# Linear attention and a gated feed-forward layer on one core: queries in two layouts, softmax statistics through DRAM

## The chip, the cores and the metric

The kernel runs on one core of a Trainium2 chip. The time is the device time of one execution in microseconds (us). The core has five instruction streams that run beside each other: TensorE (PE in the profile; its weight loads are PEld), VectorE (DVE), ScalarE (ACT), GpSimd (POOL) and SyncE (SP), which here issues all DMAs. Sixteen DMA engines move the data. Matrix products go to PSUM; everything else that is computed lies in SBUF.

## The reference

```python
def attn(q, k, v):                       # each (8, 8, 576, 64), float32
    q_s = exp(q - max(q, axis=-1));  q_s /= sum(q_s, axis=-1) + 1e-9     # over the 64 channels
    k_s = exp(k - max(k, axis=2));   k_s /= sum(k_s, axis=2) + 1e-9      # over the 576 tokens
    kv = einsum('bhsd,bhse->bhde', k_s, v)
    return einsum('bhsd,bhde->bhse', q_s, kv)

x = attn(q, k, v).transpose(0, 2, 1, 3).reshape(4608, 512)
out = ((x @ w_a) * (x @ w_b)) @ w_out    # w_a, w_b (512, 1536), w_out (1536, 512), float64
```

A query's softmax runs over channels, a key's over tokens. So where tokens lie on partitions, a query's maximum is one along the row and a key's one across partitions; where channels lie on partitions it is the other way round.

## The kernel before

The 4608 tokens are taken in nine chunks c of T = 512. Two heads at a time make a group g of 128 channels, four groups in all. A chunk has two halves of work. *Attention* gives xf[c], the chunk's input to the feed-forward layer with channels on partitions, one tile px of 128x512 per group. *The feed-forward layer* multiplies it by w_a and w_b, takes their product and multiplies that by w_out.

Each matrix is split into a high and a low part of type float32r (`split`), and three products high x high, high x low, low x high make one. From chunk 1 on, the products by w_a and w_b are made in Winograd's form: six rounds i per chunk, each of seven products (kx, ky, ka, kp; `product`, L393 to L404, twelve matmuls each), whose weights are loaded from a DRAM scratch tensor into eight buffers ws (`get_w`). Between them stand the projections by w_out of earlier rounds (`project`, po, 24 matmuls of 512 columns per round). VectorE and ScalarE empty the products (u2, u3, cc) and split the gates (gh, gl). Chunk 0 uses plain products (`gate_first`) while the float64 weights are read (raw), converted (`convert_ab`, `convert_wo`) and written to the scratch tensors dy and dw; chunk 1 also forms the sums of weights that Winograd's form needs (`sums`, `split_w`, `put_w`).

The attention of chunk c + 1 is cut into steps (`attention_tasks`) and spread over chunk c (`Spread`): a chunk's loop calls `attend()` three times a round, and each call takes the next entry of the list. A key group's step is load, softmax, product with v (kv, a 128x128 matrix per batch and group); a query group's step is load, softmax, product with kv. Each step has three parts, and an entry holds part 0 of one step, part 1 of the step before and part 2 of the one before that.

- Keys lie with tokens on partitions (kt, 128x640). The maximum over tokens is taken by three VectorE operations and then across partitions, on GpSimd (`partition_all_reduce`, L217) or, for batch 2, by a transpose, a reduce and a product with a diagonal matrix (pm, pmx, L208, L214). Batches 0 and 1 are loaded turned instead (`k_load_t`, `kv_soft_t`): a reduce along the row, an Exp with the maximum as bias, and five transposes back (L241).
- Queries lie with tokens on partitions (qt, 128x512). VectorE takes the maximum, subtracts it, ScalarE takes Exp, VectorE sums, inverts and multiplies (`q_soft`, L296 to L311; for chunk 1 `q_soft_first`, with eight Exps that sum along the way, and the multiplication on GpSimd). Four transposes turn the tile (`q_transpose`, L316, pq), ScalarE and VectorE split it from PSUM (qh, ql), up to six matmuls give px (`x_product`, L333), and ScalarE copies px into xf (L472).

The tiles pk, pq, px and the maxima share one PSUM buffer ("at"). Instructions go to the engines in an order that a scheduler of the framework makes at build time from the code's order and dependencies; each engine, SyncE too, then runs its own list in order, and an instruction that waits holds up all behind it. On SyncE each DMA also waits until the eighth DMA before it has landed.

Of the kernel before, what the change touches and what calls it, by code (L numbers as in the profile page):

```python
# [7 lines left out]
F32 = mybir.dt.float32  # L8
# [21 lines left out]
def linear_attention_then_gated_ffn(  # L30
# [4 lines left out]
    kt_first: bass.AP,  # L35
    v: bass.AP,
# [29 lines left out]
    ones = const.tile([P, P], F32, name="ones")  # L66
    nc.gpsimd.memset(ones, 1.0)
# [116 lines left out]
    def k_load(b, g, kt=None):  # L184
        if kt is None:
            kt = sb.tile([P, J, 2, D], F32, name="kt")
        nc.sync.dma_start(out=kt, in_=k[b, g])
        return kt
# [7 lines left out]
    def kv_soft(b, kt, tags=("at", "at")):  # L196

        kf = kt.rearrange("p j h d -> p j (h d)")
        m2 = sb.tile([P, 2, P], F32, name="m2", bufs=1)
        m1 = sb.tile([P, P], F32, name="m1")  # L200
        nc.vector.tensor_tensor(out=m2, in0=kf[:, 0:2], in1=kf[:, 2:4], op=ALU.max)
        nc.vector.tensor_tensor(out=m1, in0=m2[:, 0], in1=m2[:, 1], op=ALU.max)
        nc.vector.tensor_tensor(out=m1, in0=m1, in1=kf[:, 4], op=ALU.max)  # L203
        if b == 2:


            pm = ps.tile([P, P], F32, name="pm", tag=tags[0])
            nc.tensor.transpose(pm, m1, ident)  # L208
            mc = sb.tile([P, 1], F32, name="mc")
            nc.vector.tensor_reduce(out=mc, in_=pm, axis=AX.X, op=ALU.max)  # L210
            dg = sb.tile([P, P], F32, name="m1")
            nc.vector.tensor_scalar_mul(dg, ident, mc)
            mx = ps.tile([P, P], F32, name="pmx", tag=tags[1])
            nc.tensor.matmul(mx, ones, dg, start=True, stop=True)  # L214
        else:
            mx = sb.tile([P, P], F32, name="mx")
# [7 lines left out]
        return kt  # L224

    def k_load_t(b, g, kt=None):
        if kt is None:
            kt = sb.tile([P, J, P], F32, name="kt")
        nc.sync.dma_start(out=kt, in_=kt_first[b, g])
        return kt  # L230
# [41 lines left out]
    def q_load(c, g, qt=None):  # L272
        if qt is None:
            qt = sb.tile([P, TT, 2, D], F32, name="qt")
        nc.sync.dma_start(out=qt, in_=q[c, g])
        return qt

# [161 lines left out]
    def attention_tasks(c):  # L439
# [3 lines left out]
        for b in range(c * T // S, (c * T + T - 1) // S + 1):  # L443
# [3 lines left out]
            for g in range(NP):  # L447
                box = {}

                def s0(b=b, g=g, box=box):  # L450
                    box["t"] = ((k_load_t if b == 1 else k_load)(b, g), v_load(b, g))

                def s1(b=b, box=box):
                    kt = box["t"][0]
                    box["e"] = kv_soft_t(kt, ("k2", "at")) if b == 1 else kv_soft(b, kt)

                def s2(b=b, g=g, box=box):
                    kv_split(b, g, kv_product(box["e"], box["t"][1]))

                steps.append((s0, s1, s2))  # L460
        for g in range(NP):
            box = {}

            def s0(c=c, g=g, box=box):
                box["q"] = q_load(c, g)

            def s1(c=c, box=box):
                box["e"] = (q_soft_first if c == 1 else q_soft)(box["q"])

            def s2(c=c, g=g, box=box):  # L470
                px = x_product(c, g, q_transpose(box["e"]))
                nc.scalar.copy(out=xfs[c][:, g], in_=px)  # L472

            steps.append((s0, s1, s2))

        seq = []
        n = len(steps)
        for i in range(n + 2):
            now = []
            if i < n:  # L480
                now.append(steps[i][0])
# [207 lines left out]
```

## Time and profile before

| what | us |
|---|---|
| three runs | 998.41, 994.8, 995.98 (median 995.98) |
| the profiled execution | 995.74 |
| its span on the core, at a granted clock of 0.991 | 993.3 |

The execution's own time is 2.4 us longer than the span, which runs from the first instruction to the last. A line of the groups reads: source line, engine, operation, result <- operands, shapes, count; then the busy time of the group, the mean duration of one in ns, and the engine's idle time just before such instructions with what ended it. Matmuls overlap, so a mean duration is longer than the place one takes in TensorE's row. The DMA line gives tenths of all 16 engines' time in 40 slices of the span. HBM was read for 219.38 MB and written for 37.75 MB.

### The profile page before, as it was taken

Reading aid. Unit: us, or ns where it says so; the run is one execution under the profiler, and the core shown is the slowest. Engines: PE = TensorE matmul, PEld = TensorE weight load, DVE = VectorE, ACT = ScalarE, POOL = GpSimd, SP = SyncE. Lnnn points to the kernel's source line nnn. Section 1 sums busy time; section 2 is a strip of 40 time slices with the busy share of each in tenths; the row PEclk is TensorE's granted clock in tenths of the full one; section 3 lists DMA queues with packets and bytes.
Section 4 is the critical chain, followed back from the end, with each engine's and each line's share of the span. In section 5 each row is a group of like instructions: output and inputs, shape, how many; then the busy total and the mean of one; then the engine's idle time right before and its main releaser. Section 6 shows DMA issues by size and latency. Waiting matters only on the chain.

```text
span 993.3 us, 16580 instructions
## 1 busy us (share of the span) xinstructions
PE 962.1 (97%) x6276; PEld 866.0 (87%) x6276; DVE 654.0 (66%) x1280; ACT 333.5 (34%) x667; POOL 114.2 (11%) x96
## 2 busy tenths in 40 slices
PE   4889999999999999999999999999999999999998
PEld 4667666999989999999999999999999999999996
DVE  7797887887787774677468656865577555353433
ACT  7666675332342322233223212322233232121111
POOL 3344345440000000000000000000000000000000
PEclk9799998999999999999999999999999999999999
DMA  9599858978777587866796679767867676767761
GB/s 345 216 413 401 336 213 282 384 276 294 239 272 270 212 292 270 292 220 240 239 331 228 229 249 325 257 219 245 296 221 250 211 274 216 251 238 271 252 207 50
DMA packets 84605, 261.35 MB, mean 263 GB/s; under 512 B 9392, under 2 KB 9520, under 8 KB 84528
## 3 DMA queue, kind: packets, MB, share of 16 engines
q1 hardware_dynamic: 84528, 260.31, 73.8%
q8 instruction: 50, 0.82, 0.3%
q14 instruction: 27, 0.22, 0.1%
HBM read 219.38 MB, written 37.75 MB: 259 GB/s over the span
## 4 chain that ended last, share of the span: by engine, by line
PE 83%; DVE 4%; DMA 4%; issue 3%; ACT 2%; POOL 2%; SPq 0%; POOLq 0%; DVEq 0%; ACTq 0%
PE po L420 26%; PE ka L401 14%; PE kx L401 14%; PE kp L401 14%; PE ky L401 7%; PE pk L249 3%; PE px L333 2%; POOL wr L101 2%; PE pt L378 2%; PE po L410 1%; DMA wo_w<-wy 1%; PE pq L316 1%; DMA wo_raw<-in_w_out 1%; DVE ws L80 1%; DMA qt<-in_q 1%
## 5 line engine op out<-in xcount | busy, mean ns | idle before, releaser
L420 PE MATMUL po<-wo_w,gh 128*128 128x512 f32 x768 | 225.0, 394 | 1.0 <-ACT gh L77 1.0
L401 PE MATMUL kx<-xo,ws 128*128 128x256 f32 x1152 | 167.1, 285 | 0.0
L401 PE MATMUL ka<-xo,ws 128*128 128x256 f32 x1152 | 161.9, 285 | 0.2 <-ACT xo L77 0.2
L420 PEld LDWEIGHTS po<-wo_w,gh 128*128 128x128 f32 x768 | 138.4, 189 | 26.6 <-ACT gh L77 1.4
L401 PE MATMUL kp<-xo,ws 128*128 128x256 f32 x1152 | 157.4, 284 | 0.0
L401 PEld LDWEIGHTS kx<-xo,ws 128*128 128x128 f32 x1152 | 152.4, 191 | 4.0 <-ACT ws L77 0.2
L401 PEld LDWEIGHTS ka<-xo,ws 128*128 128x128 f32 x1152 | 151.3, 192 | 4.3 <-ACT xo L77 0.7
L401 PEld LDWEIGHTS kp<-xo,ws 128*128 128x128 f32 x1152 | 147.2, 191 | 1.6
L420 PE MATMUL po<-wo_w,gl 128*128 128x512 f32 x384 | 136.8, 397 | 0.0
L77 ACT CAST gh<-cc 128x512 fp32r<-128x512 f32 x96 | 58.7, 622 | 159.1 <-DVE cc L632 113.1
L631 DVE TENSOR_TENSOR cc<-kp,u 128x512 f32<-128x512 f32 x48 | 33.0, 687 | 82.3 <-PE kp L401 81.9
L420 PEld LDWEIGHTS po<-wo_w,gl 128*128 128x128 f32 x384 | 71.1, 189 | 14.8
L401 PE MATMUL ky<-xo,ws 128*128 128x256 f32 x576 | 80.1, 288 | 1.0 <-ACT xo L77 1.0
L378 PE MATMUL pt<-xo,ws 128*128 128x512 f32 x288 | 74.1, 406 | 3.9 <-ACT ga L385 3.2
L401 PEld LDWEIGHTS ky<-xo,ws 128*128 128x128 f32 x576 | 73.8, 194 | 1.6 <-ACT xo L77 1.4
L80 DVE TENSOR_TENSOR gl<-cc,gh 128x512 fp32r<-128x512 f32 x96 | 68.0, 714 | 10.1 <-ACT gh L77 10.1
L622 ACT COPY cc<-kx 128x256 f32<-128x256 f32 x48 | 17.9, 372 | 168.3 <-PE kx L401 162.9
L621 DVE TENSOR_TENSOR cc<-kp,u 128x512 f32<-128x512 f32 x48 | 33.0, 688 | 62.2 <-PE kp L401 61.9
L378 PEld LDWEIGHTS pt<-xo,ws 128*128 128x128 f32 x288 | 53.3, 188 | 20.3 <-ACT ga L385 4.6
L217 POOL PARTITION_ALL_REDUCE mx<-m x20 | 14.7, 733 | 475.1 <-DVE m L203 434.8
L410 PE MATMUL po<-wo_w,ga 128*128 128x512 f32 x96 | 43.5, 592 | 0.0
L635 DVE TENSOR_TENSOR cc<-ka,u 128x512 f32<-128x512 f32 x48 | 32.9, 685 | 15.4 <-PE ka L401 15.2
(119 smaller groups left out, 1211.0 us busy)
## 6 DMA issues: line engine op xcount, KB each, us to landing
ws<-dw SPq DMA_DIRECT2D x312, 512.0 KB, 4.7
dw<-ws SPq DMA_DIRECT2D x42, 512.0 KB, 4.7
raw<-in_w_ab SPq DMA_DIRECT2D x24, 512.0 KB, 7.9
out<-ot SPq DMA_DIRECT2D x36, 256.0 KB, 4.1
vt<-in_v SPq DMA_DIRECT2D x28, 325.0 KB, 6.1
qt<-in_q SPq DMA_DIRECT2D x32, 256.0 KB, 4.0
kt<-in_k SPq DMA_DIRECT2D x24, 320.0 KB, 4.6
wo_raw<-in_w_out SPq DMA_DIRECT2D x12, 512.0 KB, 8.1
```

What stands on the lines that cost most here:

```text
L77: nc.scalar.copy(out=hi, in_=src)
L80: nc.vector.tensor_tensor(out=lo, in0=src, in1=hi.bitcast(F32), op=ALU.subtract)
L101: nc.gpsimd.tensor_tensor(out=r, in0=u, in1=r, op=ALU.add)
L249: nc.tensor.matmul(pk, kt[:, j].rearrange("p h d -> p (h d)"), vt[:, j], start=(j == 0), stop=(j == J - 1),)
L333: nc.tensor.matmul(px[:, s], w, m[:, s], start=(i == 0), stop=(i == 2))
L378: nc.tensor.matmul(pt, w[:, wp], x[g][:, xp], start=(i == 0), stop=(i == 3 * NP - 1))
L401: nc.tensor.matmul(pt[:, n], w[:, n, wp, c], x[:, xp, c], start=(first and n == 0 and i == 0), stop=(i == 5), skip_group_check=True,)
L410: nc.tensor.matmul(po[t], g[:, t * P:(t + 1) * P], wo[f][:, 1].bitcast(F32), start=(f == 0), stop=(f == NF - 1),)
L420: nc.tensor.matmul(po[t], a[:, ts], wo[f][:, w], start=(f == 0 and i == 0), stop=(f == NF - 1 and i == 2),)
L621: nc.vector.tensor_tensor(out=cc[:, 3], in0=kp, in1=u3, op=ALU.add)
L631: nc.vector.tensor_tensor(out=cc[:, 1], in0=kp, in1=u2, op=ALU.add)
L635: nc.vector.tensor_tensor(out=cc[:, 2], in0=ka, in1=u2, op=ALU.add)
```

## The change

For all batches from 1 on, and all chunks from 1 on, softmax maxima (and the sums of queries) are now found in the layout in which they lie along a row, written to a small DRAM tensor, and read back as a broadcast into the layout in which the values are used. A query group is loaded twice, plain (qn) and turned (qt); the eight Exps over qn give only the sums. A key group is loaded twice too, turned (kr) for the maximum only and plain (kt). Chunk 0 and batch 0 stay as they were. A step has four parts now, the first of which finds the statistics. px is multiplied by the inverse sums on VectorE where ScalarE copied it.

```diff
+    def k_max(b, g):
+        kr = sb.tile([P, S], F32, name="kr", tag="nat")
+        nc.sync.dma_start(out=kr, in_=kt_rest[b - 1, g])
+        mc = sb.tile([P, 1], F32, name="mc")
+        nc.vector.tensor_reduce(out=mc, in_=kr, axis=AX.X, op=ALU.max)
+        dm = dr.tile([1, P], F32, name=f"dm{b}{g}")
+        nc.sync.dma_start(out=dm.rearrange("o p -> p o"), in_=mc)
+        mx = sb.tile([P, P], F32, name="mx")
+        nc.sync.dma_start(out=mx, in_=dm.broadcast_to([P, P]))
+        return mx
...
-    def kv_soft(b, kt, tags=("at", "at")):
+    def kv_soft(kt, mx):
         kf = kt.rearrange("p j h d -> p j (h d)")
-        m2 = sb.tile([P, 2, P], F32, name="m2", bufs=1)
...
-        if b == 2:
...
-            nc.gpsimd.partition_all_reduce(
-                out_ap=mx, in_ap=m1, channels=P, reduce_op=bass_isa.ReduceOp.max,
-            )
         nc.vector.tensor_tensor(
             out=kf, in0=kf, in1=mx.unsqueeze(1).broadcast_to([P, J, P]), op=ALU.subtract
         )
         nc.scalar.activation(out=kf, in_=kf, func=AF.Exp)
...
+    def q_stats(c, g):
+        qt = sb.tile([P, 2, TT, D], F32, name="qn", tag="nat")
         nc.sync.dma_start(out=qt, in_=q[c, g])
+        qv = qt.rearrange("p h j d -> p (h j) d")
+        st = sb.tile([P, 2, 2, TT], F32, name="st")
+        sv = st.rearrange("p w h j -> p w (h j)")
+        nc.vector.tensor_reduce(out=sv[:, 0], in_=qv, axis=AX.X, op=ALU.max, negate=True)
+        for i in range(2 * TT):
+            nc.scalar.activation(
+                out=qv[:, i], in_=qv[:, i], func=AF.Exp, bias=sv[:, 0, i:i + 1],
+                accum_out=sv[:, 1, i:i + 1],
+            )
+        nc.vector.tensor_scalar_add(sv[:, 1], sv[:, 1], EPS)
+        nc.vector.reciprocal(out=sv[:, 1], in_=sv[:, 1])
+        dq = dr.tile([2, 2, P, TT], F32, name=f"dq{c}{g}")
+        nc.sync.dma_start(out=dq.rearrange("w h p j -> p (w h) j"), in_=st.rearrange("p w h j -> p (w h) j"))
+        mr = sb.tile([P, 2, T], F32, name="mr", tag="mr")
+        for h in range(2):
+            nc.sync.dma_start(
+                out=mr[h * D:(h + 1) * D],
+                in_=dq[:, h].rearrange("w p j -> w (p j)").unsqueeze(0).broadcast_to([D, 2, T]),
+            )
+        return mr
+
+    def q_load(c, g):
+        qt = sb.tile([P, T], F32, name="qt", tag="kt")
+        nc.sync.dma_start(out=qt, in_=qt_rest[c, g])
+        return qt
+
+    def q_exp(qt, mr):
+        nc.vector.tensor_tensor(out=qt, in0=qt, in1=mr[:, 0], op=ALU.add)
+        nc.scalar.activation(out=qt, in_=qt, func=AF.Exp)
+        qh = sb.tile([P, T], F32R, name="qh", bufs=1)
+        ql = sb.tile([P, T], F32R, name="ql", bufs=1)
+        split(qh, ql, qt)
+        return qh, ql
...
-                px = x_product(c, g, q_transpose(box["e"]))
-                nc.scalar.copy(out=xfs[c][:, g], in_=px)
-
-            steps.append((s0, s1, s2))
+            def s3(c=c, g=g, box=box):
+                px = x_product(c, g, box["e"])
+                nc.vector.tensor_tensor(out=xfs[c][:, g], in0=px, in1=box["m"][:, 1], op=ALU.mult)
+
+            steps.append((s0, s1, s2, s3))
...
-        n = len(steps)
-        for i in range(n + 2):
...
+        n, parts = len(steps), 4
+        for i in range(n + parts - 1):
+            seq.append([steps[i - j][j] for j in range(parts) if 0 <= i - j < n])
```

The scheduler orders all of it anew. Three places show how.

TensorE in chunk 4, where chunk 5's first query group is made; before:

```order
L401 MATMUL ka<-xo,ws 128x256 x12
L401 MATMUL kx<-xo,ws 128x256 x4
L316 MATMUL pq<-ident,qt 128x128 x4
L401 MATMUL kx<-xo,ws 128x256 x8
L401 MATMUL ky<-xo,ws 128x256 x12
L420 MATMUL po_5280<-wo_w,gh_5556 128x512 x2
L401 MATMUL ka<-xo,ws 128x256 x12
L420 MATMUL po_5280<-wo_w,gl_5557 128x512
L420 MATMUL po_5281<-wo_w,gh_5556 128x512 x2
L420 MATMUL po_5281<-wo_w,gl_5557 128x512
L333 MATMUL px<-qh,kvh_4151 128x320
```

and now:

```order
L420 MATMUL ka<-xo,ws 128x256 x12
L352 MATMUL px<-qh,kvh_4253 128x320
L352 MATMUL px<-ql,kvh_4253 128x320
L352 MATMUL px<-qh,kvl_4254 128x320
L420 MATMUL kp<-xo,ws 128x256 x12
L420 MATMUL kx<-xo,ws 128x256 x12
L420 MATMUL ka<-xo,ws 128x256 x12
L352 MATMUL px<-qh,kvh_5442 128x192
L352 MATMUL px<-ql,kvh_5442 128x192
L352 MATMUL px<-qh,kvl_5443 128x192
L420 MATMUL ky<-xo,ws 128x256 x12
```

The four transposes pq, which stood inside the product kx, are gone; the six px of the first group stand between products as before, and nothing of the query's preparation is left on TensorE.

The second place is where chunk 2's feed-forward layer ends. ScalarE before (u, cc and gh belong to the products, ot to the stores of po, xf, qt and qh to the queries):

```order
L607 COPY u_4427<-kx 128x512
L472 COPY xf<-px 128x512
L303 ACTIVATE qt<-qt 128x512
L77 CAST qh<-pq 128x512
L622 COPY cc<-kx 128x256
L303 ACTIVATE qt<-qt 128x512
L472 COPY xf<-px 128x512
```

and now:

```order
L78 CAST gh_4019<-cc 128x512
L624 COPY u_4028<-kx 128x512
L291 ACTIVATE qt<-qt 128x512
L78 CAST gh_3999<-cc 128x512
L78 CAST qh<-qt 128x512
L268 ACTIVATE qn,st<-qn,st 128x64 x13
L451 COPY ot<-po_2975 128x512
L268 ACTIVATE qn,st<-qn,st 128x64 x3
L451 COPY ot<-po_2976 128x512
L451 COPY ot<-po_2977 128x512
L639 COPY cc<-kx 128x256
```

The copy of px into xf is gone; two bursts of eight Exps (qn, st) stand as one row of thirteen and one of three, with stores' copies and the copy of kx (L639) behind them. On SyncE before there were query loads among weight loads (ws):

```order
L275 DMA qt<-in_q 128x512
L163 DMA ws<-dw_2420 128x1024
L163 DMA ws<-dw_893 128x1024
L163 DMA ws<-dw_984 128x1024
L275 DMA qt<-in_q 128x512
L163 DMA ws<-dw_2499 128x1024
L163 DMA ws<-dw_2518 128x1024
L163 DMA ws<-dw_2549 128x1024
L163 DMA ws<-dw_998 128x1024
L275 DMA qt<-in_q 128x512
```

and now, a little further on:

```order
L275 DMA dq_5602<-st 128x4x4
L164 DMA ws<-dw_509 128x1024
L164 DMA ws<-dw_591 128x1024
L164 DMA ws<-dw_2080 128x1024
L278 DMA mr<-dq_4596 64x2x512
L164 DMA ws<-dw_2099 128x1024
L278 DMA mr<-dq_4596 64x2x512
L164 DMA ws<-dw_2165 128x1024
L200 DMA kt<-in_k 128x640
L189 DMA kr<-in_kt_rest 128x576
L275 DMA dq_5686<-st 128x4x4
```

A statistics store (dq) that waits for VectorE, the two broadcast loads (mr) of another group, and the turned keys (kr) now stand between weight loads; the query group whose store stands first is read back 27 rows behind it.

The third place is SyncE in the first stage, where the third weight block's raw loads begin; before:

```order
L126 DMA wo_w<-wy 128x512
L229 DMA kt<-in_kt 128x640
L193 DMA vt<-in_v 128x650
L114 DMA raw<-in_w_ab 128x512 x2
L118 DMA wo_raw<-in_w_out 128x512
L114 DMA raw<-in_w_ab 128x512 x2
```

and now:

```order
L195 DMA mx<-dm_524 128x128
L195 DMA mx<-dm_532 128x128
L193 DMA dm_620<-mc 128x1
L262 DMA qn<-in_q 128x512
L115 DMA raw<-in_w_ab 128x512 x2
L119 DMA wo_raw<-in_w_out 128x512
L115 DMA raw<-in_w_ab 128x512 x2
```

Ahead of the raw weights stood a load of batch 1's turned keys (kt) and of v; now there are two key maxima read back (mx), a third one written (dm), and a plain query load (qn).

More of the change, by code (lines that the diff above doesn't have):

```diff
@@ L511, in linear_attention_then_gated_ffn @@
         first.append((kt, vt, qt))
-        k_load_t(0, g, kt)
-        q_load(0, g, qt)
+        nc.sync.dma_start(out=kt, in_=kt_first[g])
+        nc.sync.dma_start(out=qt, in_=q_first[g])
         v_load(0, g, vt)
```

70 lines of the change are left out of this document (23 added, 47 removed).

## The prediction

> **What bounds the kernel now.** I read the page first: engines, slices, DMA queue, and the chain of work that ended last.
>
> ```profile
> span 993.3 us, 16580 instructions
> ...
> PE 962.1 (97%) x6276; PEld 866.0 (87%) x6276; DVE 654.0 (66%) x1280; ACT 333.5 (34%) x667; POOL 114.2 (11%) x96
> ...
> DMA  9599858978777587866796679767867676767761
> ...
> q1 hardware_dynamic: 84528, 260.31, 73.8%
> ...
> PE 83%; DVE 4%; DMA 4%; issue 3%; ACT 2%; POOL 2%; SPq 0%; POOLq 0%; DVEq 0%; ACTq 0%
> ```
>
> TensorE is busy nearly throughout and holds 83% of the chain; the 17% that is not TensorE must lie somewhere. So I cut the span into stages (columns: stage; busy time and count of PE, PEld, DVE, ACT, POOL; granted clock; DMA share; GB/s).
>
> ```profile
> 40.00:120.00 80.00, 75.76 (x307) 53.66 (x306) 62.23 (x107) 50.35 (x96) 35.77 (x25) 0.99 0.96 377
> 120.00:165.00 45.00, 44.77 (x172) 29.61 (x170) 35.79 (x51) 28.74 (x75) 24.45 (x18) 1.00 0.61 220
> 165.00:283.00 118.00, 112.81 (x761) 103.33 (x760) 97.10 (x188) 43.66 (x80) 26.75 (x18) 0.97 0.81 290
> 283.00:383.00 100.00, 100.00 (x728) 94.76 (x728) 73.21 (x163) 29.38 (x52) 4.22 (x6) 1.00 0.74 263
> 383.00:983.00 600.00, 599.47 (x4190) 560.83 (x4189) 350.43 (x697) 148.11 (x273) 9.02 (x12) 1.00 0.71 246
> ```
>
> Three stages. Up to 165 us the weights are converted and chunk 0 runs; from 40 to 120 us the DMA engines are full (0.96). Chunk 1 (to 283 us) loses 5 us of TensorE. From 283 us on TensorE never rests: 0.53 us idle in 600. Whether a full TensorE row also means full pace is told by one round of the loop without attention (two rows of the chain in the last chunk) and one with it (timeline).
>
> ```profile
> 939.88 2.80 PE po L420 x12
> ...
> 955.52 2.80 PE po L420 x12
> ```
> ```profile
> 449.15 1.60 PE L401 MATMUL kx<-xo,ws 128*128 128x256 f32 x12
> 450.59 1.28 PE L249 MATMUL pk<-vt,kt 128*128 128x130 f32 x10
> 451.63 1.68 PE L401 MATMUL ky<-xo,ws 128*128 128x256 f32 x12
> ...
> 465.89 1.60 PE L401 MATMUL kx<-xo,ws 128*128 128x256 f32 x12
> ```
>
> A bare round takes 955.52 - 939.88 = 15.64 us; a round with one key product takes 465.89 - 449.15 = 16.74. The key product takes 451.63 - 450.59 = 1.04, and 15.64 + 1.04 = 16.68. So from 283 us each piece of attention on TensorE costs just its own place in the row. What leaves TensorE there leaves the time.
>
> **The change part by part.** First what it removes from TensorE: the group of query transposes, one set of four in the timeline with its neighbours, the transposes of batch 1's keys, and a maximum of batch 2 in the chain.
>
> ```profile
> L316 PE MATMUL pq<-ident,qt 128*128 128x128 f32 x128 | 19.5, 272 | 0.8 <-ACT xf L472 0.8
> L241 PE MATMUL pka<-ident,kt 128*128 128x128 f32 x16 | 3.1, 312 | 0.2 <-ACT kt L242 0.2
> ```
> ```profile
> 440.32 1.35 PE L401 MATMUL kp<-xo,ws 128*128 128x256 f32 x10
> 441.51 0.60 PE L316 MATMUL pq<-ident,qt 128*128 128x128 f32 x4
> 441.86 0.48 PE L401 MATMUL kp<-xo,ws 128*128 128x256 f32 x2
> ```
> ```profile
> 209.04 0.49 PE pmx L214 x2
> ```
>
> The group says 272 ns each, but matmuls overlap: the next kp begins 441.86 - 441.51 = 0.35 us after the four began. I use 0.35. The 128 transposes are 32 sets. 28 of them (chunks 2 to 8) prepare the next chunk from inside the Winograd loops; all but chunk 2's four stand in the two full stages, and those four right at their edge. **28 x 0.35 = 9.8 us off the path.** Batch 2's four maxima (pm, pmx) stand in chunk 1's loop, where TensorE is 96% busy: some 4 x 0.49 = 2.0; I count half, **1.0 us**, as chunk 1 waits for other things too. The other four sets and batch 1's 20 transposes (1.4 us, and 20 x 0.09 = 1.8 at the pace of the set) fall before 165 us, where DMA and conversions set the pace; I count them at nothing. If that cover is gone they are 3 us more.
>
> The Trainium skill, "TensorE: Matmul & The Clock Gate", part 4 (PE-mode transpose), reports some 275 ns for a 128x128 transpose within a kernel. The group's 272 ns agrees as a duration, the timeline's spacing of 0.09 us does not as a cost; by the page the 28 sets would be 31 us, by the row 9.8.
>
> Second, what moves onto VectorE and ScalarE (the prices: the reduce that goes, two operations on 512 columns, one that reads PSUM, the copy that goes, and two steps of exponentials with sums).
>
> ```profile
> L305 DVE TENSOR_REDUCE qst<-qt 128x8 f32<-128x512 f32 x28 | 19.2, 685 | 14.5 <-ACT qt L303 14.3
> L308 DVE TENSOR_TENSOR qt<-qt,qst 128x512 f32<-128x512 f32 x28 | 20.4, 728 | 0.6
> L621 DVE TENSOR_TENSOR cc<-kp,u 128x512 f32<-128x512 f32 x48 | 33.0, 688 | 62.2 <-PE kp L401 61.9
> L472 ACT COPY xf<-px 128x512 f32<-128x512 f32 x32 | 18.6, 581 | 27.6 <-PE px L333 27.5
> ```
> ```profile
> 5.71 0.35 ACT L285 ACTIVATE qts<-qts,qst 128x64 f32<-128x64 f32 x1
> ...
> 6.06 0.33 ACT L285 ACTIVATE qts<-qts,qst 128x64 f32<-128x64 f32 x1
> ```
>
> Per query group VectorE loses the second reduce (0.69), keeps the first (L299, of the same size), the subtraction (now an addition) and the normalisation (now the multiplication that empties px, priced as L621): it gets lighter. ScalarE loses the copy (0.58) and gets eight exponentials at 6.06 - 5.71 = 0.35 us, 2.8 us in a row: +2.2 x 28 = 62 us on an engine that is 34% busy. Queued behind such a burst stand the copies of kx and the splits of gates. The next products into kx come at least one product and one gate's projections later (450.59 - 449.15 = 1.44, and the 2.80 of the chain's rows), so a burst of 2.8 us is covered, two bursts together not quite. I count 0 and keep +5 as the other end.
>
> Third, DMA (issues and median landing; what TensorE's buffers make SyncE wait; how the weight loads of a round go out).
>
> ```profile
> ws<-dw SPq DMA_DIRECT2D x312, 512.0 KB, 4.7
> ...
> qt<-in_q SPq DMA_DIRECT2D x32, 256.0 KB, 4.0
> ...
> ident<-in_eye SPq DMA_DIRECT2D x1, 64.0 KB, 2.0
> ```
> ```profile
> SPq L163 <- PE kp L401: 241.7, 70, 5.6
> ```
> ```profile
> 453.34 14.51 SPq L163 DMA_DIRECT2D ws<-dw  x7
> ```
> ```profile
> DMA packets 50996, 168.34 MB, mean 248 GB/s; under 512 B 5665, under 2 KB 5665, under 8 KB 50943
> ```
>
> Each of 32 query groups now also loads a second layout (256 KB) and two broadcasts (512 KB); each of 28 key groups the turned keys (288 KB) and a broadcast (64 KB): 32 x 768 + 28 x 352 KB = 35 MB. At 246 GB/s for a share of 0.71, 35 MB are 101 us of all 16 engines, ten points: 0.71 becomes 0.81. Unknown are the small pieces: the statistics of a query group go out as 128x4 runs of 16 B, key maxima as 128 of 4 B, 32 x 512 + 28 x 128 = 19,968 pieces, and no row shows such a write. From below they cost nothing; from above as much as a mean packet here, 680 us (300 to 980 us) x 16 x 0.71 / 50,996 = 0.15 us, so 188 us of the 16 engines, 19 points more: full. A piece carries 1/200 of a mean packet's bytes, so I take the lower end and keep the upper as a rival.
>
> The weight loads bear a longer landing: SyncE issues seven in 14.5 us, each as TensorE frees a buffer (241.7 us of waiting for kp alone); with eight buffers a load is used about a round after its issue, 16 us, and lands in 4.7. So **some 11 us of spare** stand behind each new wait on SyncE (a store of statistics waits for VectorE's reciprocal, its broadcast for that store to land, or for VectorE to be done with an old one). A chain of store and broadcast is two small landings, 2.0 us each at best and 8 if both are like loads.
>
> VectorE itself now waits for more loads:
>
> ```profile
> DVE qst L299 <- DMA qt<-in_q: 29.8, 23, 3.2
> DVE m L201 <- DMA kt<-in_k: 17.7, 13, 3.0
> ```
>
> These waits, up to 3.2 us, already block all that stands behind them on VectorE, and TensorE did not rest for them after 283 us. The order has the statistics written many weight loads before they are used, so I count the new ones at 0, with +5 as the bad end.
>
> Fourth, the early stages. Between the raw weights of the full stage now stand c=1's query statistics and broadcasts. All that is added for chunk 1 is 4 x 1120 KB = 4.6 MB, at 377 GB/s 12 us at worst; most of its broadcasts come late, near the emptier 120 to 165 us (0.61). Against it, two rows:
>
> ```profile
> 38.21 2.82 ACT qt L285 x17
> ```
> ```profile
> 42.29 0.33 SPq L229 DMA_DIRECT2D kt<-in_kt  x1
> 42.66 0.43 SPq L193 DMA_DIRECT2D vt<-in_v  x1
> 43.14 0.90 SPq L114 DMA_DIRECT2D raw<-in_w_ab  x2
> ```
>
> Two bursts of chunk 1's exponentials stand in the chain before 42 us (x17 is half of it, so some 5 us together) and move behind the first chunk's work; the next raw weights, which waited on SyncE behind a key load, wait for a key maximum instead. So -5 to +12; I take **+2**, because the added bytes fall into the one stage where DMA is full.
>
> **Sum:** -9.8 - 1.0 + 2 = -8.8. The profiled execution took 995.74 us (span 993.3 and 2.4 around it), so 987; the median of the runs, 995.98, is 0.2 above it.
>
> **The rivals.** *Given back* (22%): the early stage takes its full 12 us, or late weights and VectorE's waits cost a microsecond per chunk on top of a smaller loss; for it speaks the 0.96, against it the room after 120 us. -10.8 + 12 = +1: 997; with half of it 991.
> *The DMA engines become the bound* (14%): pieces cost like packets. 0.738 x 993 = 733 us of all engines, + 101 + 188 = 1022, so 1025 us. It decides from 985 - 733 - 101 = 151 us, 0.12 us a piece, earlier if the engines can't be packed full. For it: 0.71 is high already, and in the program each DMA waits until the eighth before it has landed, the small ones counted too. Against: a piece has so few bytes.
> The Trainium skill speaks for it: "DMA: Bandwidth & Descriptors", specifications and rules for kernel authors, has writes under 512 B done as read-modify-write and non-contiguous runs as one descriptor each. No run here shows either yet.
> *Bursts and waits stop TensorE* (6%): two bursts together, or a broadcast that is late on VectorE, stall products; 2.5 us for each of 28 sets less 9.8 would be +60, more likely one in four: +17.5 - 10.8, 1003. Against it, 0.53 us idle now in spite of such waits.
> *Early gain too* (6%): -10.8 - 5 - 3 = -19, 977.
> *Transposes cost their duration* (2%): 272 ns x 112 = 30 us, 965; the timeline's spacing speaks against it, the TensorE page for it.
>
> **How the numbers follow.** My forecast, 980 to 991 around 987, has 50%. About 0.5%, 5 us, is what a measurement of this kernel can tell from no change. Faster: 50 + 6 + 2 = 58%; same 22%; slower 14 + 6 = 20%. The range: from 977 (under it some 4%) to 1006 (above it the DMA bound, about 14%).
>
> **What would show it.** Right: rounds of 15.64 us plus products only, TensorE without idle time after the second chunk's start, the DMA share near 0.81, weight loads landing within 8 us, and pq gone from the groups. Wrong: idle time before kx or ky that ends with a weight load (DMA bound); VectorE idle for mx or mr over 4 us with TensorE idle behind it (waits); kx or cc copies late behind the exponentials (bursts); a DMA share near 1.0 where little is moved (pieces); the second chunk starting after 290 us (early stages).

## The result, and the profile after

The changed kernel takes **1098.2 us** (four runs, 1097.62 to 1101.38) against 996.09 of the kernel before: 1.1029 times as long, 95% interval 1.1 to 1.1058. Forecast were 987 us, with 1006 as the upper end.

The page of the changed kernel, the same lines as before (busy time of the engines, DMA in tenths by slice, the DMA queue, the chain by engine and by line):

```profile
span 1099.2 us, 16938 instructions
...
PE 976.0 (89%) x6116; PEld 868.6 (79%) x6116; DVE 635.1 (58%) x1204; ACT 389.9 (35%) x1083; POOL 91.1 (8%) x71
...
DMA  9999999999999999999999999989688877667661
...
q1 hardware_dynamic: 127344, 295.86, 90.3%
...
PE 47%; DMA 39%; DVE 5%; issue 4%; ACT 2%; POOL 1%; SPq 0%; POOLq 0%; DVEq 0%; ACTq 0%
PE po L439 16%; DMA ws<-dw 15%; PE ka L420 8%; PE kx L420 8%; PE kp L420 8%; PE ky L420 4%; DMA mr<-dq 4%; DMA qn<-in_q 3%; DMA dq<-st 2%; DMA dm<-mc 2%; DMA dw<-ws 2%; DMA kt<-in_k 2%; DMA qt<-in_q_t 2%; DMA vt<-in_v 2%; POOL wr L102 1%
```

The chain, 83% TensorE before, is now 39% DMA, and its first DMA is the weight load ws. DMA reads 9 in every slice up to the 26th of 40. The same kernel by stages (stage; busy time and count of PE, PEld, DVE, ACT, POOL; granted clock; DMA share; GB/s):

```profile
40.00:120.00 80.00, 66.80 (x251) 47.70 (x251) 57.06 (x101) 49.40 (x131) 24.95 (x17) 0.88 1.02 320
120.00:165.00 45.00, 38.85 (x135) 26.20 (x134) 35.11 (x51) 24.59 (x44) 18.15 (x13) 0.92 1.07 267
165.00:283.00 118.00, 95.29 (x547) 80.77 (x546) 85.07 (x143) 51.99 (x149) 28.38 (x20) 0.90 1.00 299
283.00:383.00 100.00, 87.24 (x569) 80.38 (x569) 57.98 (x115) 35.99 (x121) 5.89 (x4) 0.93 1.02 268
383.00:683.00 300.00, 260.24 (x1734) 239.10 (x1733) 161.75 (x340) 106.28 (x371) 0.00 (x0) 0.95 1.00 268
683.00:983.00 300.00, 296.40 (x2051) 276.24 (x2050) 160.37 (x310) 77.50 (x167) 0.00 (x0) 1.00 0.81 274
```

The rows from 383 to 683 and from 683 on tell most. In the first TensorE has lost 40 us of 300 and DMA is "full", yet it moves only 268 GB/s: the kernel before moved 377 GB/s in its first stage at a share of 0.96. In the second, TensorE is nearly full again, at a share of 0.81 and 274 GB/s. So the loss stops somewhere near 683 us. What stops there? The waits of TensorE and of SyncE name the late transfers, and the issues (count, size, median us to landing) and one tile's row name the transfer that ends there:

```profile
PE kx L420 <- DMA ws<-dw: 27.5, 10, 6.3
...
PE ka L420 <- DMA ws<-dw: 11.7, 10, 3.5
```
```profile
SPq L164 <- DMA ws<-dw: 56.5, 50, 2.9
...
SPq L164 <- DMA dm<-mc: 26.6, 8, 4.9
```
```profile
ws<-dw SPq DMA_DIRECT2D x312, 512.0 KB, 6.9
...
dq<-st SPq DMA_DIRECT2D x32, 8.0 KB, 8.5
dm<-mc SPq DMA_DIRECT2D x28, 0.5 KB, 12.0
```
```profile
L193 SPq DMA_DIRECT2D dm<-mc x28: 319/323/570, 29.0 to 624.1; - x28
```

The slowest of all transfers to land is the smallest: dm, 512 bytes, 12.0 us. The last of the 28 is issued at 624.1 us, shortly before TensorE recovers. A pair of them, and the throughput around it:

```profile
420.04 0.32 SPq L193 DMA_DIRECT2D dm<-mc  x1
...
424.22 0.32 SPq L193 DMA_DIRECT2D dm<-mc  x1
```
```profile
420.00:425.00 5.00, 4.85 (x34) 4.40 (x34) 3.79 (x10) 1.88 (x4) 0.00 (x0) 1.00 1.03 399
425.00:434.00 9.00, 8.19 (x53) 7.06 (x51) 2.84 (x8) 2.38 (x4) 0.00 (x0) 1.00 1.03 178
434.00:441.00 7.00, 3.14 (x24) 2.94 (x24) 3.76 (x9) 0.00 (x0) 0.00 (x0) 1.00 0.94 263
```

For nine microseconds the engines are as "busy" as before (1.03) and move 178 GB/s instead of 399; then TensorE is idle for 3.9 of 7 us. That is a suspicion, not yet a cause: the same stretch also has SyncE standing behind those stores, and 35 MB more to move. The experiments take them one by one.

A gap costs TensorE more than its own length here. Behind the gap of 2.17 us that ends at 441.07 us, twelve matmuls of ka take 2.87 us, at a granted clock of 0.72 from 441 to 447 us; the next twelve of ka, at 450.95 us and a clock of 1.00, take 1.60. From 165 to 690 us the clock is 0.94, in the kernel before 0.99, and TensorE is busy for longer in all (976.0 us against 962.1) with 160 matmuls fewer. So the loss is gaps and slower products together.

### The profile page after: what moved, and what is told of

The parts are those of the page before. It is cut to its first block, busy times and chain, and to the rows that moved or that the text cites. A ratio compares the mean times of both kernels' runs of the same rounds, so it can differ in the third digit from the quotient of the medians.

```text
span 1099.2 us, 16938 instructions
## 1 busy us (share of the span) xinstructions
PE 976.0 (89%) x6116; PEld 868.6 (79%) x6116; DVE 635.1 (58%) x1204; ACT 389.9 (35%) x1083; POOL 91.1 (8%) x71
## 4 chain that ended last, share of the span: by engine, by line
PE 47%; DMA 39%; DVE 5%; issue 4%; ACT 2%; POOL 1%; SPq 0%; POOLq 0%; DVEq 0%; ACTq 0%
PE po L439 16%; DMA ws<-dw 15%; PE ka L420 8%; PE kx L420 8%; PE kp L420 8%; PE ky L420 4%; DMA mr<-dq 4%; DMA qn<-in_q 3%; DMA dq<-st 2%; DMA dm<-mc 2%; DMA dw<-ws 2%; DMA kt<-in_k 2%; DMA qt<-in_q_t 2%; DMA vt<-in_v 2%; POOL wr L102 1%
## 5 line engine op out<-in xcount | busy, mean ns | idle before, releaser
L420 PEld LDWEIGHTS kx<-xo,ws 128*128 128x128 f32 x1152 | 155.6, 198 | 35.5 <-DMA ws<-dw 25.9
L420 PE MATMUL ka<-xo,ws 128*128 128x256 f32 x1152 | 166.2, 291 | 16.0 <-DMA ws<-dw 11.7
L420 PEld LDWEIGHTS ka<-xo,ws 128*128 128x128 f32 x1152 | 154.7, 197 | 21.7 <-issue 8.2
L439 PEld LDWEIGHTS po<-wo_w,gh 128*128 128x128 f32 x768 | 141.3, 192 | 28.8 <-ACT gh L78 1.7
L439 PE MATMUL po<-wo_w,gl 128*128 128x512 f32 x384 | 131.4, 395 | 3.6 <-DVE gl L81 3.6
L268 ACT ACTIVATE qn<-qn,st 128x64 f32<-128x64 f32 x256 | 85.6, 336 | 73.2 <-DVE st L266 68.8
L397 PE MATMUL pt<-xo,ws 128*128 128x512 f32 x288 | 79.2, 431 | 17.7 <-ACT ga L404 13.1
L420 PE MATMUL ky<-xo,ws 128*128 128x256 f32 x576 | 81.5, 292 | 11.9 <-DVE cc L648 5.9
L397 PEld LDWEIGHTS pt<-xo,ws 128*128 128x128 f32 x288 | 58.3, 207 | 36.9 <-ACT ga L404 16.2
L639 ACT COPY cc<-kx 128x256 f32<-128x256 f32 x48 | 17.7, 369 | 177.6 <-PE kx L420 170.1
L291 ACT ACTIVATE qt<-qt 128x512 f32<-128x512 f32 x32 | 20.2, 631 | 98.3 <-DVE qt L290 98.2
L290 DVE TENSOR_TENSOR qt<-qt,mr 128x512 f32<-128x512 f32 x32 | 23.2, 724 | 55.0 <-DMA mr<-dq 27.3
```

Of the source, the lines that this page charges most:

```text
L268: nc.scalar.activation(out=qv[:, i], in_=qv[:, i], func=AF.Exp, bias=sv[:, 0, i:i + 1], accum_out=sv[:, 1, i:i + 1],)
L290: nc.vector.tensor_tensor(out=qt, in0=qt, in1=mr[:, 0], op=ALU.add)
L291: nc.scalar.activation(out=qt, in_=qt, func=AF.Exp)
L397: nc.tensor.matmul(pt, w[:, wp], x[g][:, xp], start=(i == 0), stop=(i == 3 * NP - 1))
L420: nc.tensor.matmul(pt[:, n], w[:, n, wp, c], x[:, xp, c], start=(first and n == 0 and i == 0), stop=(i == 5), skip_group_check=True,)
L439: nc.tensor.matmul(po[t], a[:, ts], wo[f][:, w], start=(f == 0 and i == 0), stop=(f == NF - 1 and i == 2),)
```

## The experiments

Three theories were on the table. **A**: each store of key maxima, 128 pieces of 4 B, holds up the DMA engines. **B**: the added bytes, and broadcasts that all read one place. **C**: SyncE stands behind stores and loads that wait for each other. In the diffs below a minus is the changed kernel, unless said otherwise.

### Half of the change each, and the stores alone

e1 is the changed kernel with the key maxima as before (`k_load`, `k_load_t` and `kv_soft` are those of the kernel before).

```diff
-                    box["m"] = k_max(b, g)
+                    box["t"] = ((k_load_t if b == 1 else k_load)(b, g), v_load(b, g))
...
-                steps.append((s0, s1, s2, s3))
+                steps.append((s0, s1, s2, lambda: None))
```

> The changed kernel with the key maxima found as before (in SBUF and on GpSimd or TensorE, batch 1 turned by TensorE); the queries stay changed. Theory A (the 28 stores of key maxima, 128 pieces of 4 B each, hold the DMA engines): the DMA share falls from 1.0 to 0.85 or less in the loop and the time to 985 to 1000 us. Rival B (the added bytes and the broadcasts that read one place in DRAM fill the engines; 25 of 35 MB are the queries'): still 1060 to 1080. Rival C (SyncE stands behind dependent stores and loads, and weights come late): about half of the loss stays, 1030 to 1060.

e2 is the kernel before with only the key half of the change (`k_max` and the shorter `kv_soft`; minus is the kernel before).

```diff
-                    box["t"] = ((k_load_t if b == 1 else k_load)(b, g), v_load(b, g))
+                    box["m"] = k_max(b, g)
...
-                steps.append((s0, s1, s2))
+                steps.append((s0, s1, s2, s3))
...
-            steps.append((s0, s1, s2))
+            steps.append((s0, s1, s2, lambda: None))
```

> The kernel before with the key maxima passed through DRAM as in the change; queries as before. Theory A: 1060 to 1100 us, DMA share near 1.0 where the maxima are stored. Rival B (10 of 35 MB): 1000 to 1025. Rival C: 1020 to 1050.

e3 leaves out the store of the key maxima; what is subtracted from the keys is a row of them, not their maximum.

```diff
-        dm = dr.tile([1, P], F32, name=f"dm{b}{g}")
-        nc.sync.dma_start(out=dm.rearrange("o p -> p o"), in_=mc)
         mx = sb.tile([P, P], F32, name="mx")
-        nc.sync.dma_start(out=mx, in_=dm.broadcast_to([P, P]))
+        nc.sync.dma_start(out=mx, in_=kt_rest[b - 1, g][0:1, 0:P].broadcast_to([P, P]))
```

> The changed kernel without the stores of key maxima: the broadcast is read from the first 128 values of the same group's turned keys in DRAM, so that the loads stay, and what is subtracted is not the maximum. Theory A: 985 to 1005 us. Rival B: 1080 or more, as all but 14 KB of the bytes stay. Rival C: 1000 to 1030, as the broadcast waits for nothing.

e4 is e3 with the two lines of the store put back; nobody reads what is stored.

> As the run before, but the maxima are stored too, and nobody reads them or waits for them; the broadcast comes from the turned keys and what is subtracted is not the maximum. Theory A: 1080 to 1105 us, as the changed kernel. Rival B: the same. Rival C: 1000 to 1030, as with the run without the stores.

| kernel | us, median | against before (95% interval) |
|---|---|---|
| the change | 1098.2 | 1.1029 (1.1 to 1.1058) |
| e1, queries only | 1024.18 | 1.0277 (1.0253 to 1.0301) |
| e2, keys only | 1065.04 | 1.0685 (1.0622 to 1.0749) |
| e3, maxima not written | 1014.23 | 1.0176 (1.0145 to 1.0207) |
| e4, written and unread | 1078.54 | 1.0821 (1.0778 to 1.0864) |

e2 is what A expected. e1 fell between A's range and C's. e3 lies 9 us above A's range and inside C's, so it speaks against B but cannot decide between A and C. e4 does: it is 1.5 us short of A's range, and C, which gave it 1000 to 1030, is 48 us too low. The sharpest pair is e3 and e4: 28 stores of 512 bytes, which nobody reads, cost 1078.54 - 1014.23 = 64 us, 2.3 us each. The stage from 383 to 683 us, first of e3, then of e4:

```profile
383.00:683.00 300.00, 300.00 (x2116) 281.72 (x2115) 189.48 (x396) 120.81 (x396) 0.00 (x0) 1.00 0.98 320
```
```profile
383.00:683.00 300.00, 274.81 (x1829) 253.51 (x1828) 165.75 (x352) 115.12 (x407) 0.00 (x0) 0.95 1.01 277
```

e3 moves 320 GB/s at a share of 0.98, and TensorE does not rest at all. So the bytes are not what stops TensorE here (against B), and a share near 1 alone does not tell a full queue from one that is stuck. But e4 differs from e3 in two things: the pieces, and that SyncE has a store to issue and must wait for the reduce before it.

### Fewer pieces, spread pieces, wider pieces

f1 keeps e4's wait and stores one piece. f2 keeps the wait and all 128 pieces, and only puts them 512 B apart. (Minus is e4.) In both, as in e3, what is subtracted isn't the maximum.

```diff
-        nc.sync.dma_start(out=dm.rearrange("o p -> p o"), in_=mc)
+        nc.sync.dma_start(out=dm[:, 0:1], in_=mc[0:1])
```

> As e4 (the maxima written, and not read), but of the 128 maxima only the first is written: one piece of 4 B per store, behind the same reduce. Theory A (each store's 128 small pieces hold up the DMA engines): the 64 us between e3 (1014) and e4 (1078) go, 1010 to 1025. Theory C (SyncE stands behind a store that waits for VectorE's reduce): the wait is the same as in e4, so 1060 to 1080. The landing of a store under A: 2 to 4 us, where the whole change's take 12.0.

```diff
-        dm = dr.tile([1, P], F32, name=f"dm{b}{g}")
-        nc.sync.dma_start(out=dm.rearrange("o p -> p o"), in_=mc)
+        dm = dr.tile([P, P], F32, name=f"dm{b}{g}")
+        nc.sync.dma_start(out=dm[:, 0:1], in_=mc)
```

> As e4, but each of the 128 pieces of 4 B is written 512 B from the last (128 rows of a 128x128 tensor) where e4 writes them side by side in 512 B. If a small write costs by itself, wherever it goes: 1065 to 1090, as e4. If it costs because 128 writes fall on the same 512 B and take turns there: 1012 to 1030, with stores that land in 3 to 5 us.

e7 is the whole change with the column of maxima turned on VectorE, so that it leaves as four rows of 128 B.

```diff
-        mc = sb.tile([P, 1], F32, name="mc")
-        nc.vector.tensor_reduce(out=mc, in_=kr, axis=AX.X, op=ALU.max)
+        m32 = sb.tile([P, 32], F32, name="m32")
+        nc.vector.memset(m32, 0.0)
+        nc.vector.tensor_reduce(out=m32[:, 0:1], in_=kr, axis=AX.X, op=ALU.max)
+        mt = sb.tile([P, 32], F32, name="mt")
+        nc.vector.transpose(out=mt, in_=m32)
         dm = dr.tile([1, P], F32, name=f"dm{b}{g}")
-        nc.sync.dma_start(out=dm.rearrange("o p -> p o"), in_=mc)
+        nc.sync.dma_start(out=dm.rearrange("o (a p) -> (o a) p", p=32), in_=mt[0:P:32])
```

> The whole change, except that VectorE turns the column of maxima in blocks of 32 (a memset and a 32x32-block transpose of 128x32 more per key group, under 1 us of VectorE), so that they are written as 4 pieces of 128 B instead of 128 of 4 B. Everything else of the chain is kept: reduce, store, broadcast, subtraction. Theory A: e3 (1014) plus what the dependence of broadcast on store costs, 1014 to 1040. Theory C (the dependence itself): 1085 to 1100.

f1 took 1012.6 us (1.0172, 1.014 to 1.0204), f2 1015.87 (1.0189, 1.0153 to 1.0224), e7 **1011.63** (1.0144, 1.0121 to 1.0168). f1 keeps SyncE's wait for the reduce and loses the 64 us, so they were not that wait (against C). f2 tells more: as many writes, as small, and in all they cost 1.6 us against e3, which two runs of each cannot tell from nothing. The queue and the landing of the store, in e4 and in f2:

```profile
q1 hardware_dynamic: 127344, 295.86, 90.6%
...
dm<-mc SPq DMA_DIRECT2D x28, 0.5 KB, 11.9
```
```profile
q1 hardware_dynamic: 127344, 295.86, 87.4%
...
dm<-mc SPq DMA_DIRECT2D x28, 0.5 KB, 6.3
```

The same packets and bytes; the store lands in 6.3 us where e4's took 11.9. That is still longer than the 3 to 5 us expected; the landing of f1's store is not on record. (e3 has 123,312 packets, 4032 fewer, which is 28 x 144: each of the 128 pieces is a packet, with 16 more per store.) So it is neither the number of writes nor their size alone, but that they go to neighbouring places: 128 of them into the same 512 bytes. That they take turns there is how I read it; the runs show the spacing and its price.

One part of C comes back as a consequence of A. A store that lands late also holds up SyncE, since each DMA waits for the eighth before it: all its waits for dm add up to 54 us in e4 and 78 us in the change (where the broadcasts wait for it too), and there are none in f1, f2 and e7. So the 64 us can reach TensorE in two ways, over slower engines and over a queue that stands. The engines are slow in any case: from 428.3 to 433.0 us of the change SyncE stands for dm, and they show a share of 0.97 at 116 GB/s, so they are not out of work. How the 64 us divide between the two ways no run tells.

The Trainium skill, "DMA: Bandwidth & Descriptors", specifications, has writes under 512 B done as read-modify-write. By that rule alone f2's 4-byte pieces would cost what e4's cost; they cost 63 us less, so the rule names the kind of write that is in danger and the measurement adds the condition, the shared place.

e7 also shows when the 20 us between e4 and the whole change arise: the broadcast that depends on the store costs nothing that can be seen once the store is quick (e7 1011.63, e3 1014.23). With the same 35 MB and the same dependences, the whole change runs at 318 GB/s and TensorE is idle for 1.2 us in 400:

```profile
283.00:683.00 400.00, 398.82 (x2794) 373.46 (x2793) 257.57 (x552) 158.88 (x516) 0.00 (x0) 1.00 0.99 318
```

### What is left: the first stage

e7 is still 15 us slower than the kernel before. Where chunk 1 begins is seen by the first ky (timeline; kernel before, the change, e7):

```profile
169.48 0.58 PE L401 MATMUL ky<-xo,ws 128*128 128x256 f32 x1 [1.05 <-ACT xo L77]
```
```profile
196.55 0.78 PE L420 MATMUL ky<-xo,ws 128*128 128x256 f32 x2
```
```profile
181.41 0.79 PE L423 MATMUL ky<-xo,ws 128*128 128x256 f32 x2 [9.60 <-ACT ws L78]
```

27 us are lost there in the change, 12 in e7. g2 is the kernel before with 3.1 MB of loads that nobody reads in this stage; g3 makes them broadcasts of one row. (Plus is against the kernel before.)

```diff
                 box["q"] = q_load(c, g)
+                for _ in range(3 if c == 1 else 0):
+                    z = sb.tile([P, T], F32, name="z")
+                    nc.sync.dma_start(out=z, in_=q[c, g].rearrange("p j h d -> p (j h d)"))
```

> The kernel before, and each of chunk 1's four query groups loads its 256 KB three times more into a tile that nobody reads: 3.1 MB more in the first stage, no new wait but that of the DMA queue. If the 12 to 27 us that the change loses before chunk 1 are its bytes: 8 us at 377 GB/s, so 1002 to 1006. If they are waits of VectorE and SyncE on the statistics: 995 to 999.

```diff
-                    nc.sync.dma_start(out=z, in_=q[c, g].rearrange("p j h d -> p (j h d)"))
+                    nc.sync.dma_start(out=z, in_=q[c, g].rearrange("p j h d -> p (j h d)")[0:1].broadcast_to([P, T]))
```

> As g2, but the three loads broadcast one row of 2 KB to 128 partitions, as the change's broadcasts do, so that all 16 engines read one place. Bytes alone: as g2 within 2 us. If reading one place takes turns as writing one place does: 1010 to 1025.

g2 took 1004.3 us (1.0071, 1.0055 to 1.0088), g3 1004.65 (1.0075, 1.0057 to 1.0092): 8 us for 3.1 MB, as its bytes say, and reading one place costs nothing more. In g2 chunk 1 begins here:

```profile
178.09 0.58 PE L401 MATMUL ky<-xo,ws 128*128 128x256 f32 x1 [0.90 <-ACT xo L77]
```

8.6 us later than before. The change adds 4.6 MB for chunk 1, by the same rate 12 us, and e7 shows 12. This is the one stage where bytes do count. e1 starts chunk 1 later still though it adds fewer bytes, and its timeline names what e7 does not have, batch 2's maximum on TensorE:

```profile
189.51 0.79 PE L216 MATMUL pmx<-m,ones 128*128 128x128 f32 x2 [7.79 <-DVE m L214]
189.96 0.78 PE L436 MATMUL ky<-xo,ws 128*128 128x256 f32 x2
```

TensorE sat 7.79 us for VectorE's m just ahead of the first ky. Which wait stands last at this place differs from kernel to kernel (e7's ends with ACT ws), so e7's 12 us need not be bytes alone.

### Where the transposes' gain is

e5 keeps keys and chunk 1's queries as before and makes the change for the queries of chunks 2 to 8. e8 is e5 with a tile each for the two broadcasts.

```diff
-            steps.append((s0, s1, s2, s3))
+            steps.append((a0, a1, a2, lambda: None) if c == 1 else (s0, s1, s2, s3))
```

Here a0, a1 and a2 are the three query parts of the kernel before, and minus is e1; below, minus is e5.

> Keys as before (as in e1), and chunk 1's queries as before too; the queries of chunks 2 to 8 as in the change. If e1's 28 us (1024 against 996) arise in the first stage, where chunk 1's statistics and broadcasts fall among the raw weights, they go: chunk 0 ends as before, and the transposes that 7 chunks save show, 985 to 994. If the query statistics' stores and broadcasts cost in every chunk: 1000 to 1020.

```diff
-        mr = sb.tile([P, 2, T], F32, name="mr", tag="mr")
-        for h in range(2):
-            nc.sync.dma_start(out=mr[h * D:(h + 1) * D], in_=...)
+        mr = [sb.tile([P, T], F32, name=f"mr{w}") for w in range(2)]
+        for w in range(2):
+            for h in range(2):
+                nc.sync.dma_start(out=mr[w][h * D:(h + 1) * D], in_=...)
```

> As e5 (the change for the queries of chunks 2 to 8 alone), except that the broadcast of maxima and that of inverse sums have a tile each, two buffers of each, instead of sharing one pair of buffers; the same bytes in four issues of 128 KB where there were two of 256. In e5 VectorE sat for the broadcast 15.4 us between 640 and 800 us, because its buffer comes free only with the last use of the sums two groups earlier, and TensorE then waited for cc 4.6 us. If this wait eats the gain: 4 to 6 us off e5's 1000, so 994 to 996, with no idle time of TensorE before ky. If the gain is eaten by the fuller DMA engines: unchanged, 998 to 1002.

e5 took 999.92 us (1.0041, 1.0016 to 1.0066), at the edge of its second range, e8 **996.22** (0.9995, 0.9981 to 1.0008). e5's VectorE shows why (timeline near the end of a chunk):

```profile
758.60 0.68 DVE L396 TENSOR_TENSOR xt<-xf,xt 128x512 f32<-128x512 f32 x1
762.17 0.69 DVE L306 TENSOR_TENSOR qt<-qt,mr 128x512 f32<-128x512 f32 x1 [2.90 <-DMA mr<-dq]
762.78 0.68 DVE L673 TENSOR_TENSOR cc<-kp,u 128x512 f32<-128x512 f32 x1
```

VectorE waits 2.90 us for the broadcast, and cc, which frees kp's buffer, stands behind it. In e5 a broadcast's buffer comes free only when the sums in its other half have been used, two groups earlier; in e8 it does not wait for them, and the wait for mr is gone. What that cost TensorE between 640 and 800 us, in e5 and then in e8 (waits of TensorE, all of that stretch):

```profile
PE ky L436 <- DVE cc L673: 4.1, 2, 3.0
```
```profile
PE ky L437 <- DVE cc L674: 1.2, 1, 1.2
```

That is 2.9 of the some 4 us that e8 is faster. That the buffer is the cause is likely, but not shown alone: e8 also loads the broadcasts in four issues of 128 KB instead of two of 256, and VectorE still waits 13.9 us there for the turned queries (qt), where it waited 15.4 us for mr in e5. Only less of it reaches TensorE, and the sign named in advance, no idle time before ky, did not quite come. Four more runs tried to win more. h2 is e7 with the edit of e8.

> The whole change with both mends: key maxima written as 4 pieces of 128 B (e7, 1011.6) and a tile each for the broadcasts of maxima and sums (e8, which took 4 us off e5). If the two are independent: 1006 to 1009, the rest above 996 being the first stage's bytes, 8 us by g2 for the queries alone.

e9 is e8 with the statistics of a query group turned on VectorE and written as pieces of 128 B (the input qn has its tokens in another order to match).

```diff
-        st = sb.tile([P, 2, 2, TT], F32, name="st")
+        st = sb.tile([P, 4 * 2 * TT], F32, name="st")
+        nc.gpsimd.memset(st, 0.0)
...
-        dq = dr.tile([2, 2, P, TT], F32, name=f"dq{c}{g}")
+        tt = sb.tile([P, 32], F32, name="stt")
+        nc.vector.transpose(out=tt, in_=st)
+        dq = dr.tile([32, 4, 32], F32, name=f"dq{c}{g}")
+        nc.sync.dma_start(out=dq.rearrange("r a n -> a r n"), in_=tt)
```

> As e8, with a query group's statistics turned on VectorE in blocks of 32, so that they are written as 128 pieces of 128 B (half of them zeros) instead of 512 of 16 B; a memset on GpSimd and a 128x32 transpose on VectorE more per group. If 16-B pieces side by side hold up the engines as the 4-B pieces of the key maxima did, only less (some 1 to 3 us a store, seen by loads that land late): 990 to 994, and the store lands in under 5 us where it took 7.7. If not: as e8 within 2 us.

h1 and h3 are e8 with the change for the queries of chunks 4 to 8 only; h3 also gives the chunks before them three parts, as the kernel before has.

```diff
-            steps.append((a0, a1, a2, lambda: None) if c == 1 else (s0, s1, s2, s3))
+            steps.append((a0, a1, a2, lambda: None) if c < 4 else (s0, s1, s2, s3))
```

> As e8, but the queries of chunks 1 to 3 as before too: the change is left where DMA has room (the chunks whose stage showed a DMA share of 0.74 before). In e8 chunk 0 lasted 3.7 us longer than before, the chunks at a DMA share of 1.0 won nothing, and the chunks from 4 on won 1 to 2 us each. If it is the first stages' full DMA engines that ate the gain: 5 chunks x 1.4 = 7 us, so 988 to 992, faster than both kernels. If the late gain is an accident of order: 994 to 997.

```diff
-        n, parts = len(steps), 4
+        n, parts = len(steps), 3 if c < 4 else 4
```

> As h1, but the steps of chunks 1 to 3 keep three parts, as in the kernel before (h1 gave them an empty fourth). h1 lost 20 us in chunks 1 to 3, whose queries were loaded late at each chunk's end with DMA at a share of 0.51, and won 3 us in chunks 4 to 6. If the loss came with the fourth part's different order: chunks 1 to 3 as before, 990 to 994 in all, faster than both kernels by half a per cent at most. If it came with something else that h1 shares with this kernel (the tiles that queries and key maxima share): 1000 to 1010.

h2 took 1008.44 us (1.0101, 1.0078 to 1.0124): the mends add up, as far as 3 us can be told. e9 took 1000.7 (1.0038, 1.0026 to 1.005), slower than e8. That is neither of the two outcomes expected. Nothing speaks for a cost of the 16-byte pieces; but e9's memset put a new wait on GpSimd, ahead of the key maxima, so the widening's own effect can't be read from the sum, and the landing of its store is not on record:

```profile
POOL st L281 <- DVE stt L292: 126.0, 22, 11.7
```

h1 took 1008.73 (1.0111, 1.0091 to 1.0131) and h3 1000.74 (1.004, 1.0022 to 1.0058), both slower than the gain forecast. The stretch from chunk 4's first ky to chunk 7's, three chunks, of the kernel before, of e8 and of h3:

```profile
485.80:794.60 308.80, 308.80 (x2174) 289.75 (x2173) 197.23 (x405) 83.69 (x152) 6.21 (x8) 1.00 0.74 253
```
```profile
486.10:791.70 305.60, 304.41 (x2124) 284.90 (x2124) 180.01 (x365) 78.28 (x144) 8.15 (x9) 1.00 0.83 284
```
```profile
495.90:799.30 303.40, 302.24 (x2106) 282.74 (x2105) 174.51 (x349) 76.43 (x142) 7.47 (x8) 1.00 0.81 280
```

The gain is there: 3.2 and 5.4 us in three chunks. The stretches do not hold quite the same work: the kernel before has 56 transposes in it (14 sets, 4.9 us at 0.35) and 96 matmuls of key products (pk), e8 has 102 of these and h3 83. At 0.104 us for each pk (1.04 for ten) the gains become 3.8 and 4.0. The fuller DMA engines of this stretch (0.83 and 0.81) leave most of the transposes' gain. h3 has it after a start of chunk 4 that is 10 us late (495.90 against 485.80), e8 after a start 0.3 us late. h1 lost 5.9 us of TensorE at the end of one chunk with DMA half empty:

```profile
260.00:290.70 30.70, 24.76 (x143) 21.41 (x142) 19.18 (x38) 11.48 (x22) 0.00 (x0) 0.94 0.51 173
```

So it was not full DMA engines there. VectorE waited for query loads (2.90 us at 269 us, for one issued at 264.5) that SyncE had issued late: in that loop it issues the four at 254.6 to 285.2 us, the kernel before at 245.7 to 272.9. In h3 they go out at 247.0 to 274.1 and chunk 2 begins at 283.2 us, 1.3 later than before, so the late order of this loop came with the fourth part. That is not all: h3's time lies in the second range of its expectation. Its loss comes in chunks 2 and 3: there TensorE waits 7.7 us before ky for VectorE's cc, in four places, and in the kernel before in none. What delays cc there is left open. No version here beats the kernel before; e8 equals it.

## Why the prediction was wrong, point by point

- **Small pieces at nothing: the step that failed.** It said that a piece carries 1/200 of a mean packet's bytes (true of the 16-byte ones; a 4-byte one carries 1/800), "so I take the lower end". The 3584 pieces of 4 B cost 64 us by themselves (e4 less e3) and 87 us in the whole change (1098.2 less 1011.63): 2.3 to 3.1 us for each store. Bytes were the wrong measure. The rival "the DMA engines become the bound", with 14%, looked at the right place and spread its price evenly: 0.15 us of one engine for each of 19,968 pieces, 1025 us in all. In the runs nearly all of it is the 4-byte pieces': e3 keeps all of the 16-byte ones, and TensorE does not rest in 300 us. If all 16 engines stand for 2.3 us, a 4-byte piece costs 2.3 x 16 / 128 = 0.29 us of one engine, and where the pieces lie apart (f2) nothing that can be told. Both signs by which it was to be known came true: idle time before kx that ends with a weight load, and a share near 1.0 where little is moved (1.03 at 178 GB/s).
- **SyncE's waits, covered by 11 us of spare.** Right once the stores are quick (e7), wrong with them: a store of 12.0 us holds the queue, since each DMA waits for the eighth before it, and SyncE stood 26.6 us for dm ahead of weight loads, 78 us in all. In e4 it was 16.6 and 54 us; that this difference is the 20 us between e4 and the change fits, but is not shown.
- **Early stage, +2 taken, +12 as the end.** Mis-sized: without the slow stores it is the upper end, 12 us (e7; g2 puts some 8 of them down to bytes of the queries). With them it is 27, outside the bounds.
- **Transposes, -9.8.** The mechanism was right. From chunk 2's first ky to chunk 7's, the kernel before and e7:

```profile
281.90:794.60 512.70, 512.48 (x3630) 481.66 (x3630) 339.01 (x711) 142.86 (x257) 13.24 (x18) 1.00 0.74 257
```
```profile
302.40:810.20 507.80, 502.35 (x3516) 470.01 (x3516) 312.23 (x652) 182.99 (x555) 0.00 (x0) 1.00 0.94 305
```

  TensorE has 10.1 us less work and the stretch is 4.9 us shorter: 5.2 us come back as idle time. The kernel before has 88 transposes in its row, 22 sets, 7.7 us at 0.35. It also has 31 matmuls of key products more, some 3.2 us, which e7 makes at another time; so the 4.9 us are not the transposes' alone, and from chunk 4 on e7 is only 0.7 us shorter (308.1 against 308.8). The Trainium skill's 275 ns for a transpose ("TensorE: Matmul & The Clock Gate", part 4) would make it 24 us for these 88; TensorE's work fell by 10.1 us with all that changed, so the spacing of 0.09 us in a full row is the nearer price.
- **VectorE's new waits, 0 taken, +5 as the end.** The end was about right: e8 took 4 us off e5, 2.9 of them in TensorE's waits for a cc that had stood behind a late broadcast.
- **Exponentials of ScalarE, 0.** No run took them apart; in e3, with all of them, TensorE did not rest in 300 us.
- **35 MB more, share 0.71 to 0.81.** Too low: e7 shows 0.86 at 283 GB/s from 383 to 983 us, where the kernel before had the 0.71, and 0.94 in the row above. That this does no harm by itself held: TensorE loses 5 us in that row, and to VectorE.

## What to carry to other kernels

Before a column of 128 values goes from 128 partitions to DRAM, look at where its pieces land: side by side they cost microseconds of all DMA engines, and a turn of the column on VectorE, or a spacing of 512 B, takes that away. (f2 never reads its spaced values back; what that would cost is not measured.) Read the GB/s beside a DMA share: 0.98 at 320 GB/s let TensorE run at full pace, 1.00 at 268 did not. A stage that is short of DMA pays for each added byte, and here a removed instruction paid back only where nothing new stood in an in-order queue.

## What the hardware showed

- 128 writes of 4 B side by side landed in 11.9 us and cost 2.3 us of kernel time each time (e4); 512 B apart they landed in 6.3 us and cost nothing that can be told (f2).
- Around such stores transfers slowed down: 178 GB/s over 9 us where 399 stood just before, at an unchanged share of 1.03.
- Broadcasts that read one row of 2 KB 128 times cost what plain loads of the size cost (g3 1004.65, g2 1004.3).
- Behind a gap of 2.17 us twelve matmuls took 2.87 us where 1.60 is usual, at a granted clock of 0.72.
